# Row maxima of q, k, v and an expert's weights queued one to two ticks later in a fused attention, MoE and GLU kernel

## Chip, cores and metric

The kernel runs on one core of one Trainium2 chip. Its time is the device time in microseconds (us), as the median of several runs. A trace of one profiled execution shows the engines: PE (TensorE matmuls; PEld its weight loads), DVE (VectorE), ACT (ScalarE), POOL (GpSimd) and SP (SyncE, which issues most DMAs here).

## What is computed

The reference is block-causal attention (4 batches, 8 heads, 576 positions, head size 64, blocks of 64), then a mixture of 8 experts whose gate matrix is balanced by 8 row and column normalisations, then a gated unit with silu:

```python
scores = scale * np.matmul(q, k.transpose(0, 1, 3, 2))      # masked by blocks of 64
attn = np.exp(scores - max); attn /= attn.sum(-1)
x = (attn @ v) as (2304, 512)
P = exp(x @ w_gate - max), normalised 8 times over rows and columns
out = sum over e of P[:, e:e+1] * (np.maximum(x @ w1[e], 0) @ w2[e])
g = out @ w_gate2
return (silu(g) * (out @ w_val)) @ w_out
```

## The kernel before

The whole computation is one program. float32 operands of the big products are split into a high and a low float16 part, after a scaling by a power of two that comes from the operand's largest magnitude. The attention phase fills about the first 375 us; the experts' first products (L537) and their weights are already worked on in its gaps. The rest of the program is MoE and GLU.

**Ticks.** A batch has four pairs of heads, so there are 16 pairs p, and each pair has eight ticks u (`NTK = 8`). The generator `attention()` walks over `tk = 8 p + u` and yields three times in a tick; between yields the caller puts in steps of the MoE. In a tick PE makes the scores `s_p_u` (L931 for the first four pairs in float32, L942 from pair 4 on in float16), DVE takes their maxima and makes the bias (L954, L963), ACT one tick later takes the exponentials (L971), DVE two ticks later the reciprocal of the sums (L986 to L991) and POOL scales (L996), PE four ticks later transposes (L1028, copied by ACT at L1029) and then multiplies by v (L1046).

**What is listed at a tick.** A dictionary `events` lists other work by tick, and `at(tick, f, ...)` appends to it. What is listed at a tick is written into the program at the tick's start, ahead of its scores. Every engine runs its instructions in the order in which they are written. For a pair p from 4 on, with r = 8 p, these are listed:

- `load_qk` (L867): SP issues the loads of q (at r-14) and of k (r-13) into `qk0` and `qk1`; each has one buffer, so a load waits until the pair before has done its `lo_qk`.
- `max_qk` (L880): DVE reduces each to a column of magnitudes (r-11 and r-9), and L103 spreads the columns on a diagonal, `qk_d`.
- `across_mid` (L110): PE multiplies the diagonal by ones, which lays the column out as a row in a PSUM bank, `qk_a`. This is the row of maxima.
- `scale_qk` (L116 and behind): DVE reduces the row, gives the bank back, and works out the powers of two.
- `hi_qk` (ACT, L895) and `lo_qk` (DVE, L899): the high and the low part, into `hl0` (q) and `hl1` (k), one buffer each. Behind each `lo_qk` SP issues four DMAs that lay both parts out for the scores: `st0` for q (L910), `st1` for k (L912). The scores of tick r read both.

The scores of u = 0 to 6 and the rows take their PSUM banks in turn from one pool of three, so each takes the bank that was used three takings earlier and waits until that one has been read; u = 7 and the products with v have another bank.

v of the batches after the first is loaded once ahead of its use to find its maximum (`vs`, L831, reduced at L843). The rows of the experts' weights (`w_a`) are written by `across_made` when a caller asks for them and `calm` allows. In the main loop a background generator `w0` works on the first expert's weights and spends a credit of 129 a step.

```python
at(r - 6 + 2 * i, hi_qk, p, i)
at(r - 5 + 1 * i, lo_qk, p, i)
at(r - 8, lambda p: across_mid(st[p]["m"]), p)
at(r - 7, scale_qk, p)
```

Of the kernel before, what the change touches and what calls it, by code (L numbers as in the profile page):

```python
# [30 lines left out]
def attention_moe_glu_kernel(  # L31
# [66 lines left out]
    def across_begin(mx, n, name):  # L98
        pool = pairs[0] if name[0] in "qv" else small
        tag = "dgw" if name[0] == "w" else f"dg{n}"  # L100
        d = pool.tile([P, n, P], F32, tag=tag, name=f"{name}_d", bufs=1)
        for i in range(n):
            nc.vector.tensor_scalar_mul(d[:, i], ident, mx[:, i : i + 1])  # L103
        return {"d": d, "n": n, "name": name}

    def across_mid(g):
        bank, g["free"] = spread[0](g["name"])
        n = g["n"]
        g["row"] = bank[:, : n * P].rearrange("p (n q) -> p n q", n=n)
        nc.tensor.matmul(  # L110
            bank[:, : n * P], ones, g["d"].rearrange("p n q -> p (n q)"), start=True, stop=True
        )
# [8 lines left out]


    soon, row_out, calm, WAIT = [False], [False], [True], 4

    def across_soon(g):
        def mid():
            if "row" not in g and row_out[0]:
                later(1, mid)
            elif "row" not in g:
                across_mid(g)  # L130
                row_out[0] = True

        if soon[0]:
            later(WAIT, mid)

    def across_made(g):
        def made(force):
            if "row" not in g and (force and not row_out[0] or not soon[0] and calm[0]):
                across_mid(g)
                row_out[0] = True  # L140
            return "row" in g

        return made
# [22 lines left out]
    def pow2_scale(mx, n, top, name, root=False):  # L166


        g = across_begin(mx, n, name)
        across_mid(g)  # L170
        return pow2_end(g, n, top, name, root)
# [627 lines left out]
    NTK = len(TICKS)  # L799
# [5 lines left out]
    def attention(actx):  # L805
# [6 lines left out]
        vs, vmx, vt, qk, st, et, xf = {}, {}, {}, {}, {}, {}, {}  # L812
# [7 lines left out]
        def where(p):  # L820
            return p // NPAIR, ORDER[p % NPAIR]
# [3 lines left out]
        def load_v(b, hp, tag, bufs=1):  # L825
            t = tag
            if isinstance(tag, str):
                t = ap.tile([P, NJ, P], F32, tag=tag, name=f"{tag}_{b}_{hp}", bufs=bufs)
            cols = slice(hp * P, (hp + 1) * P)
            nc.gpsimd.memset(t[S - nf * P :, nf], 0.0)  # L830
            nc.sync.dma_start(t[:, :nf], v[b, : nf * P, cols].rearrange("(j p) d -> p j d", p=P))  # L831
            nc.sync.dma_start(t[: S - nf * P, nf], v[b, nf * P :, cols])
            return t
# [80 lines left out]
        def scores(p, u):  # L914
            g = st[p]
            if u == 0:
                for x in ("negm", "bias", "sum", "r"):
                    g[x] = small.tile([P, NC + 1], F32, tag=x, name=f"{x}_{p}")
            if u == NTK - 1:
                sp = ps_x.tile([P, 512], F32, tag="x", name=f"s_{p}_{u}")  # L920
            else:
                sp = ps_s.tile([P, 512], F32, tag="s", name=f"s_{p}_{u}")
            col, places = 0, []
            for c, k0, k1 in TICKS[u]:
                ps = sp[:, col : col + k1 - k0]
                col += k1 - k0
                places.append((c, k0, k1, ps, c if k0 == 0 else NC))
                if p < DIRECT:
                    for h in range(2):
                        a = slice(h * D, (h + 1) * D)  # L930
                        nc.tensor.matmul(  # L931
                            ps[h * CB : (h + 1) * CB],
                            g["q"][a, c * CB : (c + 1) * CB],
                            g["k"][a, k0:k1],
                            start=True,
                            stop=True,
                        )
                    continue
                qs, ks = g["qs"], g["ks"]
                for i in range(2):  # L940
                    for h in range(2):
                        nc.tensor.matmul(  # L942
                            ps[h * CB : (h + 1) * CB],
                            qs[:, h, c * CB : (c + 1) * CB],
                            ks[:, h, i, k0:k1],
                            start=i == 0,
                            stop=i == 1,
                        )
            g["places", u] = places
# [81 lines left out]
        def rest(p):  # L1031

            t = ps_x.tile([P, 512], F32, tag="x", name=f"t_{p}_r").rearrange("p (j q) -> p j q", q=P)
            return self_transpose(p, NC - 1, 4, t)
# [78 lines left out]
        def work(n):  # L1113
            for _ in range(min(n, len(pend))):
                pend.popleft()()

        events = {}

        def at(tick, f, *a):
            events.setdefault(tick, []).append(lambda: f(*a))  # L1120

        for p in range(1, npairs):
            r = p * NTK
            if p < DIRECT:
                if p > 1:
                    at(r - NTK, load_direct, p)
                    at(r - 2, lambda p: vt.update({p: load_v(*where(p), "v", 2)}), p)
                continue
            for i in range(2):
                if p > 1:  # L1130
                    at(r - 14 + 1 * i, load_qk, p, i)
                at(r - 11 + 2 * i, max_qk, p, i)
                at(r - 6 + 2 * i, hi_qk, p, i)
                at(r - 5 + 1 * i, lo_qk, p, i)
            at(r - 8, lambda p: across_mid(st[p]["m"]), p)
            at(r - 7, scale_qk, p)
            at(r - 2, lambda p: vt.update({p: load_v(*where(p), "v", 2)}), p)
        for b in range(B):
            r = (b - 1) * NPAIR * NTK
            for i in range(NPAIR):  # L1140
                if b:
                    at(r + i * NTK + 3, scan_load, b, i)
                at(r + i * NTK + 6 if b else 1 + i, scan_max, b, i if b else ORDER[i])
            r = r + NPAIR * NTK - 2 if b else NPAIR
            at(r, scale_v_begin, b)
            at(r + 1, lambda b: across_mid(vmx[b]), b)
            at(r + 2, scale_v_end, b)

        load_direct(0)
        for p in range(2):  # L1150
# [7 lines left out]
        def on(k):  # L1158
            return 0 <= k < tot

        for tk in range(tot + NTK):
            p, u = divmod(tk, NTK)
            calm[0] = 0 < u < 5
            for f in events.pop(tk, ()):
                f()
            if on(tk):
                scores(p, u)
            if u == 6 and p < npairs:
                take(p, 0, values(p, 0))
            yield  # L1170
            out1 = None
            if on(tk - 4):
                out1 = transposes(*divmod(tk - 4, NTK))
            work(2 if len(pend) > 6 else 1)
            if on(tk - 2):
                normalise(*divmod(tk - 2, NTK))
            if out1:
                out1()
            if on(tk):
                maxima(p, u)  # L1180
            yield

            if p and u == 4:
                work(len(pend))
                take(p - 1, 1, values(p - 1, 1))
                st.pop(p - 1)
                vt.pop(p - 1)
                if p % NPAIR == 0:
                    work(len(pend))
                    ready[0] = p // NPAIR * S // 2  # L1190
            if p and u == 3:
                rest(p - 1)()
            if on(tk - 1):
                exps(*divmod(tk - 1, NTK))
            yield
# [66 lines left out]
    with tc.manual_schedule():  # L1262
# [29 lines left out]
        w0 = Background(0)  # L1292
# [36 lines left out]
        rate, owed, wowed = 47, 0, -9 * 68  # L1329
        with ExitStack() as actx:  # L1330
            yp = actx.enter_context(tc.tile_pool(name="yp", bufs=1))
            for _ in attention(actx):
                wowed += 68
                while wowed >= 3 * 43:
                    w0.step()
                    wowed -= 3 * 43
                if ready[0]:
                    owed += rate
                    while owed >= 3 * NTK * NPAIR:
                        next(fill, None)  # L1340
                        owed -= 3 * NTK * NPAIR
            for _ in fill:
                pass
# [411 lines left out]
```

## Time and profile before

| | |
|---|---|
| median of 3 runs | 2083.08 us (2082.96 to 2089.5) |
| the profiled execution | 2082.69 us, of which the span from its first to its last instruction is 2080.9 us |
| PE busy, over the span | 1954.3 us (94%) |
| DVE busy, over the span | 1618.8 us (78%) |
| ACT busy, over the span | 1379.1 us (66%) |
| mean granted TensorE clock | 0.984 of full speed |

Positions in the rows are microseconds from the span's start. Busy shares over the span are means over very different stretches: in the attention phase neither PE nor DVE is at 94%, as the rows of its stretches below show.

### The profile page before, as it was taken

To read this page: it belongs to the slowest core of one execution; us is meant where nothing else is said; L and a number is where in the kernel's file an instruction comes from. 1 tells how busy PE (TensorE), PEld (TensorE's weight loads), DVE (VectorE), ACT (ScalarE), POOL (GpSimd) and SP (SyncE) were. 2 spreads that over 40 slices of the span, in tenths; PEclk is the share of its full clock that TensorE was granted. 3 is DMA by queue.
4 is the path that set the end of the run, shared out by engine and by line. 5 is a ranking of instruction groups with operands and counts; after the bars stand their busy time and mean duration, and the time that the engine had idled before them with its cause. 6 is when DMAs were issued, how large, how long until landed. Compare 5 with 4: busy or idle time off the path is not lost.

```text
span 2080.9 us, 47230 instructions
## 1 busy us (share of the span) xinstructions
PE 1954.3 (94%) x18378; PEld 1675.8 (81%) x18378; DVE 1618.8 (78%) x3455; ACT 1379.1 (66%) x2940; POOL 611.4 (29%) x871
## 2 busy tenths in 40 slices
PE   7779899799999999999999999999999988999998
PEld 3456666698888888888888888888888877988887
DVE  8886765668887887878878888888887877666666
ACT  6665666348777877777777777777776565544442
POOL 4534444002333333333333333333332223000000
PEclk9799999899999999999999999999999999999999
DMA  4333341306677867878678787777877100301112
GB/s 149 101 101 101 93 116 36 122 22 123 128 173 155 174 127 133 179 150 176 126 134 178 148 173 138 157 152 148 174 149 164 37 11 1 87 22 37 47 42 52
DMA packets 167505, 235.82 MB, mean 113 GB/s; under 512 B 16368, under 2 KB 84464, under 8 KB 167280
## 3 DMA queue, kind: packets, MB, share of 16 engines
q0 software_dynamic: 66560, 107.37, 30.9%
q1 hardware_dynamic: 100720, 125.42, 19.8%
q8 instruction: 144, 2.36, 0.5%
q14 instruction: 81, 0.66, 0.1%
HBM read 90.39 MB, written 24.38 MB: 55 GB/s over the span
## 4 chain that ended last, share of the span: by engine, by line
PE 56%; DVE 15%; ACT 4%; DMA 3%; issue 3%; SPq 0%; POOL 0%; DVEq 0%; ACTq 0%
PE abc_m_b L537 11%; PE m_o_b L645 11%; PE m_o_ac L645 8%; PE abc_m_c L537 5%; PE abc_m_a L537 3%; PE m_go_b L645 3%; PE abc_g_b L537 3%; PE abc_v_b L537 3%; PE m_go_ac L645 2%; DVE m_t L704 2%; DMA wr<-in_w_dram 2%; DVE m_h L193 2%; PE abc_v_c L537 1%; PE abc_g_c L537 1%; DVE w L182 1%
## 5 line engine op out<-in xcount | busy, mean ns | idle before, releaser
L537 PEld LDWEIGHTS <-w 128*128 128x128 f16 x6720 | 610.7, 99 | 111.5 <-issue 46.4
L645 PEld LDWEIGHTS <-m_h 128*128 128x128 f16 x5292 | 514.0, 98 | 68.0 <-issue 9.5
L537 PE MATMUL abc_m_b<-xs,w 128*128 128x256 f16 (+1 forms) x3840 | 478.2, 264 | 31.9 <-DVE m_t L559 29.0
L1444 POOL DMA_DIRECT2D acc<-ev x351 | 305.5, 899 | 584.2 <-ACT ev L1448 365.5
L645 PE MATMUL m_o_b<-w,m_h 128*128 128x256 f16 x3024 | 403.4, 273 | 7.7 <-ACT ev L1448 7.5
L645 PE MATMUL m_o_ac<-w,m_h 128*128 128x256 f16 x2268 | 309.4, 273 | 0.0
L537 PE MATMUL abc_m_c<-xs,w 128*128 128x256 f16 (+1 forms) x1920 | 229.9, 262 | 2.5 <-DVE m_h L758 1.4
L1448 ACT ACTIVATE ev<-m_o_b,pe 128x256 f32<-128x256 f32 x351 | 161.7, 476 | 64.2 <-PE m_o_b L645 52.9
L1448 ACT ACTIVATE ev<-m_o_ac,pe 128x256 f32<-128x256 f32 (+1 forms) x234 | 135.6, 580 | 47.8 <-PE m_o_ac L645 46.4
L178 ACT ACTIVATE w<-wr,ws 128x512 f16<-128x512 f32 x210 | 150.5, 723 | 14.5 <-DVE ws L163 10.7
L182 DVE SCALAR_TENSOR_TENSOR w<-wr,ws,w 128x512 f16<-128x512 f32 x210 | 156.0, 750 | 1.4 <-ACT w L178 1.4
L683 ACT CAST m_h<-m_t 128x512 f16<-128x512 f32 (+1 forms) x210 | 121.8, 580 | 41.6 <-DVE m_t L704 40.7
L1432 POOL DMA_DIRECT2D acc<-ev_s x65 | 73.6, 1132 | 257.0 <-ACT ev_s L1428 257.0
L676 ACT ACTIVATE m_h<-m_t 128x512 f16<-128x512 f32 (+1 forms) x210 | 121.9, 582 | 36.3 <-DVE m_t L574 25.4
L193 DVE TENSOR_TENSOR m_h<-m_t,m_h 128x512 f16<-128x512 f32 (+1 forms) x210 | 133.0, 634 | 8.7 <-ACT m_h L683 8.3
L680 DVE SCALAR_TENSOR_TENSOR m_h<-m_t,m_h 128x512 f16<-128x512 f32 (+1 forms) x210 | 132.1, 634 | 5.8 <-ACT m_h L676 5.6
L537 PEld LDWEIGHTS <-gg_w 128*128 128x128 f16 x1260 | 114.0, 98 | 21.3 <-issue 9.4
L645 PEld LDWEIGHTS <-g_h 128*128 128x128 f16 x1134 | 111.8, 99 | 20.0 <-issue 5.7
L996 POOL TENSOR_SCALAR e<-e,r 128x64 f32<-128x64 f32 (+2 forms) x144 | 77.6, 545 | 159.7 <-DVE r L991 92.7
L537 PEld LDWEIGHTS <-gv_w 128*128 128x128 f16 x1260 | 113.6, 98 | 12.7 <-issue 1.2
L537 PE MATMUL abc_m_a<-xs,w 128*128 128x256 f16 (+1 forms) x960 | 117.5, 262 | 0.0
L600 PEld LDWEIGHTS <-m_h 128*128 128x128 f16 x864 | 83.2, 99 | 16.1 <-issue 6.8
(299 smaller groups left out, 3369.1 us busy)
## 6 DMA issues: line engine op xcount, KB each, us to landing
acc<-ev POOLq DMA_DIRECT2D x351, 256.0 KB, 4.3
wr<-in_w_dram SPq DMA_DIRECT2D x128, 256.0 KB, 4.4
acc<-ev_s POOLq DMA_DIRECT2D x52, 256.0 KB, 4.2
st<-hl SPq DMA_DIRECT2D x48, 144.0 KB, 3.4
raw_g<-in_w_gate_dram SPq DMA_DIRECT2D x12, 512.0 KB, 4.9
raw_v<-in_w_val_dram SPq DMA_DIRECT2D x12, 512.0 KB, 4.6
raw_o<-in_w_out_dram SPq DMA_DIRECT2D x12, 512.0 KB, 4.7
scr_g<-gg SPq DMA_DIRECT2D x21, 256.0 KB, 3.1
```

The costliest lines, as they stand in the source:

```text
L178: nc.scalar.activation(hi, src, AF.Copy, scale=s)
L182: nc.vector.scalar_tensor_tensor(lo, src, s, hi, op0=ALU.mult, op1=ALU.subtract)
L193: nc.vector.tensor_sub(lo, src, hi)
L537: nc.tensor.matmul(ps[:, f], W[o][:, sh, k, f * P : (f + 1) * P], xs[:, o, mh, k, c0 : c0 + n], start=x not in begun, stop=True, skip_grou ...
L600: nc.tensor.matmul(p[:, c * TB : (c + 1) * TB], h[t, r][:, sh, k, ii * P : (ii + 1) * P], W[r, c][:, mh, k], start=c == 0 and j == 0, stop ...
L645: nc.tensor.matmul(ps, h[o][:, sh, k, ii * P : (ii + 1) * P], W[o][:, mh, k], start=o in (X11, X12) and k == 0 and j == 0, stop=True, skip ...
L676: nc.scalar.activation(hi, src, AF.Relu)
L680: nc.vector.scalar_tensor_tensor(lo, src, 0.0, hi, op0=ALU.max, op1=ALU.subtract)
L683: nc.scalar.copy(hi, src)
L996: nc.gpsimd.tensor_scalar(et[c][:, :n], et[c][:, :n], g["r"][:, c : c + 1], 1.0, op0=ALU.mult, op1=ALU.mult)
L1444: nc.gpsimd.dma_start(acc[:, x], e, accum_op=ALU.add)
L1448: nc.scalar.activation(e[:, cols], ps, AF.Copy, scale=p)
```

## The change

Everything that is listed for a pair from the row of maxima on goes one tick later: the row from r-8 to r-7, `scale_qk` from r-7 to r-6, `hi_qk` from r-6 and r-4 to r-5 and r-4, `lo_qk` from r-5 and r-4 to r-4 and r-3. The loads of q and k and their maxima stay where they were. For v of the later batches the row and what is behind it also go one tick later, and the load of `vs` is listed four ticks sooner (except the very first). A row of an expert's weights is now written no earlier than six yields (two ticks) after its diagonal, and no longer in tick 1 of a pair. The credit of `w0` is capped, and a step that can do nothing no longer spends any.

```diff
--- before.py
+++ after.py
@@ -101,7 +101,7 @@
         d = pool.tile([P, n, P], F32, tag=tag, name=f"{name}_d", bufs=1)
         for i in range(n):
             nc.vector.tensor_scalar_mul(d[:, i], ident, mx[:, i : i + 1])
-        return {"d": d, "n": n, "name": name}
+        return {"d": d, "n": n, "name": name, "born": yields[0]}
 
     def across_mid(g):
         bank, g["free"] = spread[0](g["name"])
@@ -121,6 +121,7 @@
 
 
     soon, row_out, calm, WAIT = [False], [False], [True], 4
+    yields = [0]
 
     def across_soon(g):
         def mid():
@@ -135,7 +136,9 @@
 
     def across_made(g):
         def made(force):
-            if "row" not in g and (force and not row_out[0] or not soon[0] and calm[0]):
+            if "row" not in g and (
+                force and not row_out[0] or not soon[0] and calm[0] and yields[0] >= g["born"] + 6
+            ):
                 across_mid(g)
                 row_out[0] = True
             return "row" in g
@@ -1130,21 +1133,21 @@
                 if p > 1:
                     at(r - 14 + 1 * i, load_qk, p, i)
                 at(r - 11 + 2 * i, max_qk, p, i)
-                at(r - 6 + 2 * i, hi_qk, p, i)
-                at(r - 5 + 1 * i, lo_qk, p, i)
-            at(r - 8, lambda p: across_mid(st[p]["m"]), p)
-            at(r - 7, scale_qk, p)
+                at(r - 5 + i, hi_qk, p, i)
+                at(r - 4 + i, lo_qk, p, i)
+            at(r - 7, lambda p: across_mid(st[p]["m"]), p)
+            at(r - 6, scale_qk, p)
             at(r - 2, lambda p: vt.update({p: load_v(*where(p), "v", 2)}), p)
         for b in range(B):
             r = (b - 1) * NPAIR * NTK
             for i in range(NPAIR):
                 if b:
-                    at(r + i * NTK + 3, scan_load, b, i)
+                    at(r + i * NTK + (3 if b == 1 and i == 0 else -1), scan_load, b, i)
                 at(r + i * NTK + 6 if b else 1 + i, scan_max, b, i if b else ORDER[i])
             r = r + NPAIR * NTK - 2 if b else NPAIR
             at(r, scale_v_begin, b)
-            at(r + 1, lambda b: across_mid(vmx[b]), b)
-            at(r + 2, scale_v_end, b)
+            at(r + (2 if b else 1), lambda b: across_mid(vmx[b]), b)
+            events.setdefault(r + (3 if b else 2), []).insert(0, lambda b=b: scale_v_end(b))
 
         load_direct(0)
         for p in range(2):
@@ -1160,7 +1163,7 @@
 
         for tk in range(tot + NTK):
             p, u = divmod(tk, NTK)
-            calm[0] = 0 < u < 5
+            calm[0] = 1 < u < 5
             for f in events.pop(tk, ()):
                 f()
             if on(tk):
@@ -1330,9 +1333,9 @@
         with ExitStack() as actx:
             yp = actx.enter_context(tc.tile_pool(name="yp", bufs=1))
             for _ in attention(actx):
-                wowed += 68
-                while wowed >= 3 * 43:
-                    w0.step()
+                yields[0] += 1
+                wowed = min(wowed + 68, 6 * 43)
+                while wowed >= 3 * 43 and w0.step():
                     wowed -= 3 * 43
                 if ready[0]:
                     owed += rate
```

Line numbers of the changed kernel are 1 higher behind the first edit and 3 higher behind the third: L899 becomes L902, L910 becomes L913, L942 becomes L945. All engines keep the order of their instructions behind the attention phase.

**The queue of SP, ahead of the scores of pair 9.** The names carry the pair: `st0_9` is q of pair 9 for the scores, `st1_9` its k, `qk0_10` and `qk1_10` are the loads of q and k of pair 10, `y0` goes with the gate's work, and `vs_3_0` is later v. Before:

```order
L867 DMA qk0_10_2531<-in_qT_dram 128x576 [waits DMAHW6_49,DVE_49]
L910 DMA st0_9_2562<-hl0_9_2529 64x576 [waits DMAHW7_49,PE_49]
L910 DMA st0_9_2562<-hl0_9_2529 64x576 [waits DMAHW0_49]
L910 DMA st0_9_2562<-hl0_9_2529 64x576 [waits DMAHW1_49]
L910 DMA st0_9_2562<-hl0_9_2529 64x576 [waits DMAHW2_49]
L867 DMA qk1_10_2567<-in_kT_dram 128x576 [waits DMAHW3_49,DVE_49]
L831 DMA vs_3_0_2569<-in_v_dram 128x4x128 [waits DMAHW4_49,Pool_49]
L832 DMA vs_3_0_2569<-in_v_dram 64x128 [waits DMAHW5_49]
L1317 DMA y0_86<-y_10_2527 128x512 [waits DMAHW6_49]
L912 DMA st1_9_2613<-hl1_9_2610 64x1152 [waits DMAHW7_49]
```

Now:

```order
L834 DMA vs_3_0_2361<-in_v_dram 128x4x128 [waits DMAHW5_49,DVE_49]
L835 DMA vs_3_0_2361<-in_v_dram 64x128 [waits DMAHW6_49]
L1320 DMA y0_86<-y_9_2382 128x512 [waits DMAHW7_49,DVE_49]
L870 DMA qk0_10_2533<-in_qT_dram 128x576 [waits DMAHW0_49,DVE_49]
L870 DMA qk1_10_2565<-in_kT_dram 128x576 [waits DMAHW1_49,DVE_49,Activation_49]
L1320 DMA y0_86<-y_10_2521 128x512 [waits DMAHW2_49]
L913 DMA st0_9_2605<-hl0_9_2563 64x576 [waits DMAHW3_49,PE_49]
L913 DMA st0_9_2605<-hl0_9_2563 64x576 [waits DMAHW4_49]
L913 DMA st0_9_2605<-hl0_9_2563 64x576 [waits DMAHW5_49]
L913 DMA st0_9_2605<-hl0_9_2563 64x576 [waits DMAHW6_49]
L915 DMA st1_9_2656<-hl1_9_2610 64x1152 [waits DMAHW7_49]
```

Both loads of pair 10 now stand ahead of the four DMAs of `st0_9`; the load of k stood between the DMAs of `st0_9` and those of `st1_9`. `vs_3_0` stands ahead of all of them. The load `qk1_10` waits in both for DVE's `hl1_9`, which reads the buffer that it fills.

**DVE at the low part of k of pair 9.** `hl1_9` is that low part, `qm_10` the maximum of q of pair 10, which was and is listed three ticks ahead of pair 9. Before:

```order
L899 SCALAR_TENSOR_TENSOR hl1_9_2610<-qk1_9_2152,qk9_s_2471,hl1_9_2610 128x576 [waits DMAHW6_49,DMAHW1_49,DMAHW7_49,DMAHW0_49,Activation_49]
L990 TENSOR_SCALAR r_8_2428<-sum_8_2427 128x1
L991 RECIPROCAL r_8_2428<-r_8_2428 128x1 [waits DVE_49]
L954 TENSOR_REDUCE negm_8_2425<-s_8_4_2618 128x1 [waits PE_49]
L963 TENSOR_SCALAR bias_8_2426<-negm_8_2425,sc_8_2061 128x1 [waits DVE_49]
L1088 TENSOR_TENSOR xf0_6_1_2257<-xf0_6_1_2257 128x5x32 [waits Pool_49]
L193 TENSOR_TENSOR xs_79<-xf1_7_1_2645,xs_79 128x160 [waits Activation_49] x2
L193 TENSOR_TENSOR xs_79<-xf0_6_1_2257,xs_79 128x160 [waits Activation_49]
L880 TENSOR_REDUCE qm_10_2661<-qk0_10_2531 128x1 [waits DMAHW6_49]
```

Now:

```order
L902 SCALAR_TENSOR_TENSOR hl0_9_2563<-qk0_9_2118,qk9_s_2528,hl0_9_2563 128x576 [waits DMAHW4_49,DMAHW5_49,DMAHW3_49,Activation_49]
L993 TENSOR_SCALAR r_8_2414<-sum_8_2413 128x1 [waits Activation_49]
L994 RECIPROCAL r_8_2414<-r_8_2414 128x1 [waits DVE_49]
L957 TENSOR_REDUCE negm_8_2411<-s_8_4_2612 128x1 [waits PE_49]
L966 TENSOR_SCALAR bias_8_2412<-negm_8_2411,sc_8_2116 128x1 [waits DVE_49]
L1091 TENSOR_TENSOR xf0_6_1_2251<-xf0_6_1_2251 128x5x32 [waits Pool_49]
L196 TENSOR_TENSOR xs_79<-xf1_7_1_2639,xs_79 128x160 [waits Activation_49] x2
L196 TENSOR_TENSOR xs_79<-xf0_6_1_2251,xs_79 128x160 [waits Activation_49]
L902 SCALAR_TENSOR_TENSOR hl1_9_2610<-qk1_9_2150,qk9_s_2528,hl1_9_2610 128x576 [waits DMAHW6_49,DMAHW1_49,DMAHW0_49]
L883 TENSOR_REDUCE qm_10_2661<-qk0_10_2533 128x1 [waits DMAHW0_49]
```

The low part of q (`hl0_9`) has taken the place of the low part of k, and `hl1_9` stands one tick further down, directly ahead of the maximum of `qm_10`.

**DVE at the first ticks of pair 9.** `s_9_0` and `s_9_1` are its scores of u = 0 and 1, `qk10_a` the row of maxima of pair 10. Before:

```order
L954 TENSOR_REDUCE negm_9_2794<-s_9_0_2798 128x1
L963 TENSOR_SCALAR bias_9_2795<-negm_9_2794,sc_9_2474 128x2 [waits DVE_49]
L116 TENSOR_REDUCE qk10_r_2833<-qk10_a_2792 128x2
L155 TENSOR_SCALAR qk10_e_2835<-qk10_r_2833 128x2 [waits DVE_49]
L162 TENSOR_SCALAR qk10_i_2837<-qk10_e_2835 128x2 [waits DVE_49]
L163 RECIPROCAL qk10_s_2838<-qk10_i_2837 128x2 [waits DVE_49]
L889 TENSOR_SCALAR sc_10_2841<-qk10_i_2837 128x1
L986 TENSOR_SCALAR r_8_2428<-sum_8_2427 128x1 [waits Activation_49]
L991 RECIPROCAL r_8_2428<-r_8_2428 128x1 [waits DVE_49]
L954 TENSOR_REDUCE negm_9_2794<-s_9_1_2843 128x1 [waits PE_49]
L954 TENSOR_REDUCE negm_9_2794<-s_9_1_2843 128x1
L963 TENSOR_SCALAR bias_9_2795<-negm_9_2794,sc_9_2474 128x2 [waits DVE_49]
```

Now:

```order
L957 TENSOR_REDUCE negm_9_2796<-s_9_0_2800 128x1
L966 TENSOR_SCALAR bias_9_2797<-negm_9_2796,sc_9_2531 128x2 [waits DVE_49]
L989 TENSOR_SCALAR r_8_2414<-sum_8_2413 128x1 [waits Activation_49]
L994 RECIPROCAL r_8_2414<-r_8_2414 128x1 [waits DVE_49]
L957 TENSOR_REDUCE negm_9_2796<-s_9_1_2837 128x1 [waits PE_49]
L957 TENSOR_REDUCE negm_9_2796<-s_9_1_2837 128x1
L966 TENSOR_SCALAR bias_9_2797<-negm_9_2796,sc_9_2531 128x2 [waits DVE_49]
L116 TENSOR_REDUCE qk10_r_2868<-qk10_a_2835 128x2
```

The reduction of the row (L116), which gives its bank back, stood ahead of the reciprocal at L986 and of the maxima of `s_9_1`, and now stands behind them. On PE the row itself has gone from directly ahead of `s_9_0` to directly ahead of `s_9_1`, and `s_9_2` now takes its bank.

## Rows read from the trace of the kernel before

**Rows 1.** Windows of the attention phase: us, then busy us (instructions) by engine, clock.

```profile
52.00:104.00 52.00, 38.57 (x251) 21.31 (x251) 43.32 (x140) 31.59 (x85) 27.51 (x60) 0.77 0.36 101
...
156.00:208.00 52.00, 49.36 (x470) 36.17 (x470) 34.72 (x122) 31.17 (x85) 24.47 (x59) 1.00 0.35 101
```

**Rows 2.** Waits of PE, 15 to 364 us: total us, times, longest.

```profile
PE w_a L110 <- DVE r L990: 5.9, 1, 5.9
...
PE qk_a L110 <- DVE qk_d L103: 4.1, 4, 1.9
PE qk_a L110 <- DVE r L990: 4.0, 3, 2.1
...
PE v_a L110 <- DVE r L990: 2.8, 1, 2.8
PE w_a L110 <- DVE w_d L103: 1.6, 2, 1.0
```

**Rows 3.** Waits of DVE, the same stretch.

```profile
DVE hl L899 <- ACT hl L895: 8.5, 10, 2.4
...
DVE vmx L843 <- DMA vs<-in_v_dram: 4.5, 3, 2.0
```

**Rows 4.** Windows across the longest wait of PE, columns as in the first group.

```profile
124.00:127.00 3.00, 0.08 (x1) 0.00 (x0) 2.46 (x6) 1.24 (x5) 0.65 (x2) 1.00 0.84 214
127.50:134.00 6.50, 4.07 (x22) 2.68 (x23) 5.69 (x20) 2.33 (x4) 0.69 (x1) 0.50 0.00 0
```

**Rows 5.** Timeline of SP ahead of pair 9: start, us, line, operation, tiles, count.

```profile
195.09 0.34 SPq L867 DMA_DIRECT2D qk<-in_kT_dram  x1
...
197.31 0.58 SPq L1317 DMA_DIRECT2D y<-y  x1
197.93 2.39 SPq L912 DMA_DIRECT2D st<-hl  x4
```

**Rows 6.** Issue to landing of the DMAs of L912, 190 to 205 us.

```profile
DMA to landing us min/median/max: 2.8/2.8/2.9
```

**Rows 7.** Timeline of DVE around the same place; in brackets idle before and its releaser.

```profile
194.25 0.82 DVE L899 SCALAR_TENSOR_TENSOR hl<-qk,qk_s,hl 128x576 f16<-128x576 f32 x1 [0.77 <-ACT hl L895]
...
198.03 0.74 DVE L880 TENSOR_REDUCE qm<-qk 128x1 f32<-128x576 f32 x1
...
204.51 0.42 DVE L116 TENSOR_REDUCE qk_r<-qk_a 128x2 f32<-128x256 f32 x1
...
207.97 0.33 DVE L963 TENSOR_SCALAR bias<-negm,sc 128x2 f32<-128x2 f32 x1
```

**Rows 8.** Timeline of PE at the first ticks of pair 9.

```profile
203.50 0.37 PE L942 MATMUL s<-st,st 128*64 128x64 f16 x8
...
207.40 0.46 PE L942 MATMUL s<-st,st 128*64 128x320 f16 x4
```

**Rows 9.** Timeline of DVE, where the low part of k of pairs 7, 10, 11, 13 will stand.

```profile
146.68 0.74 DVE L880 TENSOR_REDUCE qm<-qk 128x1 f32<-128x576 f32 x1
...
216.18 0.74 DVE L880 TENSOR_REDUCE qm<-qk 128x1 f32<-128x576 f32 x1
...
237.76 0.74 DVE L880 TENSOR_REDUCE qm<-qk 128x1 f32<-128x576 f32 x1
...
289.17 0.74 DVE L880 TENSOR_REDUCE qm<-qk 128x1 f32<-128x576 f32 x1
```

**Rows 10.** Timeline of PE, first scores of these pairs (of 10 the row ahead).

```profile
153.01 0.36 PE L942 MATMUL s<-st,st 128*64 128x64 f16 x8
...
224.62 0.70 PE L110 MATMUL qk_a<-qk_d,ones 128*128 128x256 f32 x2 [2.06 <-DVE r L990]
...
244.07 0.37 PE L942 MATMUL s<-st,st 128*64 128x64 f16 x8
...
294.20 0.37 PE L942 MATMUL s<-st,st 128*64 128x64 f16 x8
```

**Rows 11.** Waits of SP, 15 to 364 us.

```profile
SPq L867 <- DVE hl L899: 91.7, 10, 17.2
```

## Prediction

> **What bounds the kernel now.** The edits reach only the attention phase: all engines keep the order of their instructions behind it. So I read that phase alone, and what its end moves by is what the kernel moves by. I began with windows along it. In 52 to 104 us DVE is busy for 43.32 of 52 us (83%), PE for 38.57 us, and at a granted clock of 0.77; in 156 to 208 us PE is busy for 49.36 us (95%) at full clock and DVE for 34.72 us (67%) [rows 1]. So the early stretch follows DVE, and from about pair 7 on PE sets the pace: there a microsecond that PE waits is a microsecond of the kernel, and a microsecond that DVE saves is none.
>
> Next I read what PE waits for. The row matmuls of L110 wait in all for 5.9 + 4.1 + 4.0 + 2.8 + 1.6 = 18.4 us [rows 2], nearly a third of it in one place, the row of an expert's weights that ends at 129.9 us. PE waits there because the row is written directly behind the DVE instructions that make its diagonal. DVE waits too: 8.5 us for the high part that ACT writes in the same tick, and 4.5 us for `vs` to land [rows 3]. Then I read the queue of SP, since `lo_qk` feeds the scores through eight DMAs, and there lies what I think decides. SP stands for 91.7 us in ten waits at a load of L867 until DVE has done a low part [rows 11]; nothing behind it is issued in that time.
>
> **The change part by part.** Durations are from the profiled execution (2082.69 us, 0.4 us below the median of 2083.08), and the sum is made against its time.
>
> *Rows later: a gain.* The diagonal is done a tick before its row is wanted, so I take the waits of L110 for gone. What they are worth depends on the stretch. Of the 18.4 us, 5.9 lie at the weights' row. In 124 to 127 us, while PE stands, DVE is busy for 2.46 of 3.0 us [rows 4]: the wait is DVE's work and much of it comes back elsewhere. Its bounds are 0 and 5.9; I take 3.2, a little over half. Of the other 12.5 us, some 7 lie ahead of 104 us, in the stretch in which DVE is at 83%. Bounds 0 and 7; I take 1.5, about the part of DVE's own 13.0 us of waits (8.5 + 4.5) that can fall on four of twelve pairs and isn't filled with other work. The rest lies directly ahead of first scores from pair 7 on, and is settled below, with what takes its place. Gain: 4.7 us.
>
> *Low parts later: the load of k in front of the scores' DMAs.* This is the rule of the queue that I weigh most. Before, SP issued the four DMAs of `st0`, then the load of the next pair's k, then those of `st1`. Now the load of k stands ahead of all eight, and it still waits for DVE's low part of k, one tick later than before. So no DMA of q either leaves until the low part of k is done, though q's was ready a tick earlier. From the start of `hl1_9`, the last DMA lands after: the low part 0.82 us [rows 7], the load of k 0.34 and some 0.1 to the next [rows 5], four of `st0` at the length that the four of `st1` show, 2.39, three more of `st1` 1.8 [rows 5], and 2.8 to landing [rows 6]. That is 8.25 us; where a `y` of 0.58 us [rows 5] stands among them (pairs 9 and 13), 8.85.
>
> Its start is about that of the L880 beside it, which had that place before. Against the first scores of the pair:
>
> - pair 9: 198.03 [rows 7] + 8.85 = 206.9; PE wanted it at 203.50 [rows 8]: 3.4 us late
> - pair 13: 289.17 [rows 9] + 8.85 = 298.0; wanted at 294.20 [rows 10]: 3.8 late
> - pair 11: 237.76 [rows 9] + 8.25 = 246.0; wanted at 244.07 [rows 10]: 1.9 late
> - pair 7: 146.68 [rows 9] + 8.25 = 154.9; wanted at 153.01 [rows 10]: 1.9 late
> - pair 10: 216.18 [rows 9] + 8.25 = 224.4. PE stood ready 2.06 us ahead of 224.62, waiting for the row [rows 10], so at 222.6: 1.9 late, in place of the 2.06 that goes. Net nothing. I take pair 14 for the same, by its like place in a batch.
>
> At the other pairs I find the DMAs in time, or late by less than the row's wait that goes. The sum is 3.4 + 3.8 + 1.9 + 1.9 = 11.0 us. DVE no longer waits for ACT ahead of the low part (0.77 us at pair 9 [rows 7]), so it may begin up to 0.8 sooner at each of the four, which leaves 7.8. I take the middle, 9.4 us. The same DMAs were in time before because half of them had left a tick earlier.
>
> The Trainium skill speaks against this change here: its page DMA: Bandwidth & Descriptors (Anatomy of one DMA) says that DMA engines don't wait on semaphores, and that every such wait stands on the issuing sequencer, ahead of the dispatch. The 91.7 us of SP at L867 agree with it [rows 11]. If a waiting load let those behind it pass, this term would be near nothing, and the sum about 2083.
>
> *The row's bank.* `s_9_2` now takes the bank of the row, and L116, which gives it back, stands behind the bias of u = 1. That bias ended at 207.97 + 0.33 = 208.30, and with L116's 0.42 the bank is back at 208.72 [rows 7], while PE took up `s_9_2` at 207.40 [rows 8]: 1.3 us late. Where the first scores already waited for DMAs (pairs 7, 9, 11, 13), the exponentials that DVE waits for in front of that bias are done meanwhile, and little is left. At pairs 10 and 14 I take the whole, at the other eight 0.3 each, for this is worth nothing where DVE is ahead or the pace is its own: 2 × 1.3 + 8 × 0.3 = 5.0. Bounds are 0 and 12 × 1.3 = 15.6; the one row that I have belongs to a pair where it is mostly hidden, so I stay nearer the low one.
>
> *The rest.* `vs` is issued four ticks sooner, and DVE's 4.5 us go; they are among the 13.0 above. Its two DMAs take room on SP's queue ahead of the loads, where SP only waits (the 91.7 us cover them; without that cover the two would cost about 1 us a pair). The maxima of q may wait for a load that now leaves only a tick sooner; PE has work in that time. The credit and the rule on `calm` move steps of the first expert's weights inside the phase: the same instructions, so 0, with 2 us either way.
>
> Sum: 2082.7 − 4.7 + 9.4 + 5.0 = 2092.4, and with the 0.4 to the median 2092.8.
>
> **The rivals.**
>
> *The waits go and nothing takes their place: faster.* DVE loses 13.0 us of waits, so it may come to the listed tick earlier against PE than the rows say; it decides from the point at which its lead at pairs 9 and 13 has grown by 3.4 to 3.8 us. Then the DMAs are in time, and L110's waits are gain. In full that is 2083.1 − 18.4 = 2064.7; as part of them lies in DVE's stretch, half of it, 2083.1 − 9.2 = 2074, is what I would expect. For it: DVE waits for much beside PE. Against it: from pair 7 on DVE's position follows PE's scores, whose maxima it takes, so both shift together and the distance stays.
>
> *Gain and loss cancel: no change.* With the bank at nothing and the DMAs at the low end: 2083.1 − 4.7 + 7.8 − (up to 4 from waits of PE for ACT that a stall makes shorter) = 2082 to 2086. For it: a stall of PE lets ACT and DVE catch up.
>
> *The clock follows the stalls: much slower.* After the wait of 5.9 us the granted clock was 0.50 for 6.5 us, that is 1.2 in place of 2.4 GHz, and PE was busy for 4.07 us of them [rows 4]: about 2.0 us of work lost. Should each of the four stalls bring such a stretch, 4 × 2.0 = 8 come on top: 2101; with every term at its upper bound about 2110. The Trainium skill (TensorE: Matmul & The Clock Gate, What's actually happening) has activity alone release the clock, and idle time bring it back to 1.2 GHz, which the fall after 124 us bears out; whether a stall of 3.4 us is enough no row here settles.
>
> **How the numbers follow.** A measurement of this kernel can tell 0.3%, 6.2 us, from no change. I give the forecast (2088 to 2098) 0.42, the clock 0.13, cancelling 0.22 and faster 0.23. The likeliest gives 2092.8. The range reaches from 2072, which leaves out some 0.1 at the fast end, to 2104, which leaves out less than 0.1. Slower by over 0.3% (beyond 2089.3) holds most of the forecast and the clock: 0.51. Within 0.3%: the cancelling case and the edges of its neighbours, 0.28. Faster: 0.21.
>
> **What would show it.** Right: L110 hardly waits; PE's first scores of pairs 7, 9, 11 and 13 wait for `st` DMAs, by 1.9 to 3.8 us; on SP the DMAs of `st0` and `st1` leave in one run behind the load of k; `s_10_2` waits for L116. Wrong in the gain: PE still stands at L110, or DVE's busy share in 52 to 104 us does not rise. Wrong in the loss: the last `st` lands ahead of the first scores' place, or PE's stalls are made good by shorter waits for ACT behind them. The end of the attention phase against 375 us tells the sum, for nothing behind it has moved.

## The result, and the profile after

The changed kernel takes 2104.16 us (median; 2103.55 to 2108.48) against 2083.08 us of before (2082.93 to 2091.99): slower by 21 us, a ratio of 1.0106 with a 95% interval from 1.0087 to 1.0125. The forecast was 2092.8 us, in 2072 to 2104. The direction was right and the size about half. The profiled execution of the changed kernel took 2108.48 us, with a span of 2106.7 us; that of before took 2082.69 us, so the two traces lie 25.8 us apart, some 5 us more than the medians.

All of it comes out of the attention phase. The first store of the experts' output is a mark behind that phase; this is its row before and after (line, count, duration, and the first and the last start):

```profile
L1444 POOL DMA_DIRECT2D acc<-ev x351: 847/856/1549, 475.5 to 1596.3; - x176
```

```profile
L1447 POOL DMA_DIRECT2D acc<-ev x351: 847/856/1549, 503.1 to 1621.7; - x176
```

The first store starts 27.6 us later and the last 25.4 us later: what is lost is there at 503 us, and the rest of the program gives back only 2. The windows of the changed kernel:

```profile
52.00:104.00 52.00, 34.19 (x232) 17.65 (x230) 38.59 (x129) 29.54 (x82) 24.68 (x53) 0.77 0.28 77
156.00:208.00 52.00, 45.97 (x395) 33.81 (x394) 33.49 (x106) 26.89 (x75) 19.83 (x49) 0.93 0.34 90
```

In 52 to 104 us DVE, which set the pace there, fell from 43.32 to 38.59 us of work; in 156 to 208 us PE did 45.97 in place of 49.36 us, at a granted clock of 0.93 where it had been 1.00 [rows 1]. The waits of PE in the attention phase (total us, times, longest):

```profile
PE s L945 <- DMA st<-hl: 24.5, 14, 3.1
...
PE qk_a L110 <- ACT e L974: 5.3, 1, 5.3
...
PE s L945 <- DVE qk_r L116: 2.1, 4, 0.7
...
PE w_a L110 <- ACT e L974: 0.6, 1, 0.6
PE v_a L110 <- DVE r L993: 0.5, 1, 0.5
```

The row matmuls wait for 6.4 us where they waited for 18.4 [rows 2]; in their place the scores wait for 24.5 us for the DMAs of `st`, of which the kernel before has none among its waits. They lie at the first scores of eight pairs, in two pieces each at six of them (start, duration; in brackets idle before, and its releaser):

```profile
77.32 0.23 PE L945 MATMUL s<-st,st 128*64 128x64 f16 x1 [2.29 <-DMA st<-hl]
78.52 0.48 PE L945 MATMUL s<-st,st 128*64 128x64 f16 x7 [0.96 <-DMA st<-hl]
...
110.95 0.21 PE L945 MATMUL s<-st,st 128*64 128x64 f16 x1 [2.73 <-DMA st<-hl]
112.29 0.50 PE L945 MATMUL s<-st,st 128*64 128x64 f16 x7 [1.13 <-DMA st<-hl]
...
164.71 0.19 PE L945 MATMUL s<-st,st 128*64 128x64 f16 x1 [3.09 <-DMA st<-hl]
166.19 0.50 PE L945 MATMUL s<-st,st 128*64 128x64 f16 x7 [1.28 <-DMA st<-hl]
...
220.12 0.21 PE L945 MATMUL s<-st,st 128*64 128x64 f16 x1 [2.92 <-DMA st<-hl]
221.41 0.50 PE L945 MATMUL s<-st,st 128*64 128x64 f16 x7 [1.08 <-DMA st<-hl]
221.84 1.46 PE L540 MATMUL abc_m_c<-xs,w 128*128 128x256 f16 x6
...
266.37 0.19 PE L945 MATMUL s<-st,st 128*64 128x64 f16 x1 [2.49 <-DMA st<-hl]
267.68 0.50 PE L945 MATMUL s<-st,st 128*64 128x64 f16 x7 [1.12 <-DMA st<-hl]
...
320.87 0.19 PE L945 MATMUL s<-st,st 128*64 128x64 f16 x1 [2.94 <-DMA st<-hl]
322.14 0.50 PE L945 MATMUL s<-st,st 128*64 128x64 f16 x7 [1.08 <-DMA st<-hl]
```

These are pairs 4, 5, 7, 9, 11 and 13; pairs 10 and 14 waited once each, for 0.45 and 0.98 us. Early in the phase DVE has a new wait as well, for the weights' loads, which stand behind the run of eight DMAs on SP:

```profile
DVE wmx L378 <- DMA wr<-in_w_dram: 6.2, 2, 4.8
```

On DVE and SP the chain of pair 9 reads as it was forecast. DVE first, then SP:

```profile
212.53 0.86 DVE L902 SCALAR_TENSOR_TENSOR hl<-qk,qk_s,hl 128x576 f16<-128x576 f32 x1
```

```profile
213.46 0.33 SPq L870 DMA_DIRECT2D qk<-in_kT_dram  x1
213.84 0.42 SPq L1320 DMA_DIRECT2D y<-y  x1
214.35 2.43 SPq L913 DMA_DIRECT2D st<-hl  x4
216.83 2.52 SPq L915 DMA_DIRECT2D st<-hl  x4
```

The load of k leaves when the low part of k is done, and then all eight DMAs of `st` in one run; the second piece of PE's wait ends at 221.41, 8.9 us after the low part began (8.85 in the forecast). Behind the stall the clock falls:

```profile
219.00:225.60 6.60, 4.40 (x25) 3.44 (x26) 0.65 (x3) 1.99 (x5) 0.28 (x1) 0.54 0.57 150
```

That is 1.2 GHz for nearly all of 6.6 us, and six matmuls like those that took 0.82 us at 216.39 take 1.46 at 221.84.

### The profile page after: what moved, and what is told of

It is laid out like the page before. It is cut to its first block, busy times and chain, and to the rows that moved or that the text cites. A ratio compares the mean times of both kernels' runs of the same rounds, so it can differ in the third digit from the quotient of the medians.

```text
span 2106.7 us, 47220 instructions
## 1 busy us (share of the span) xinstructions
PE 1960.0 (93%) x18378; PEld 1679.4 (80%) x18378; DVE 1621.2 (77%) x3455; ACT 1379.0 (65%) x2940; POOL 613.5 (29%) x871
## 4 chain that ended last, share of the span: by engine, by line
PE 54%; DVE 16%; ACT 4%; issue 3%; DMA 3%; SPq 0%; POOL 0%; DVEq 0%; ACTq 0%
PE abc_m_b L540 11%; PE m_o_b L648 11%; PE m_o_ac L648 8%; PE abc_m_c L540 5%; PE abc_m_a L540 3%; PE abc_g_b L540 3%; PE abc_v_b L540 3%; PE m_go_b L648 3%; PE m_go_ac L648 2%; DVE m_t L707 2%; DVE m_h L196 2%; DMA wr<-in_w_dram 2%; PE abc_v_c L540 1%; DVE w L185 1%; PE abc_g_c L540 1%
## 5 line engine op out<-in xcount | busy, mean ns | idle before, releaser
L648 PEld LDWEIGHTS <-m_h 128*128 128x128 f16 x5292 | 514.0, 98 | 68.3 <-issue 9.8
L185 DVE SCALAR_TENSOR_TENSOR w<-wr,ws,w 128x512 f16<-128x512 f32 x210 | 156.1, 752 | 1.5 <-ACT w L181 1.5
L648 PEld LDWEIGHTS <-g_h 128*128 128x128 f16 x1134 | 110.4, 98 | 18.4 <-issue 5.4
L378 DVE TENSOR_REDUCE wmx<-wr 128x1 f32<-128x512 f32 x128 | 85.7, 680 | 19.1 <-DMA wr<-in_w_dram 19.0
```

Of the source, the lines that this page charges most:

```text
L185: nc.vector.scalar_tensor_tensor(lo, src, s, hi, op0=ALU.mult, op1=ALU.subtract)
L378: nc.vector.tensor_reduce(g["mx"][:, k : k + 1], g["b"][k // 2][k % 2], axis=AX.XY, op=ALU.max, apply_absolute_value=True)
L648: nc.tensor.matmul(ps, h[o][:, sh, k, ii * P : (ii + 1) * P], W[o][:, mh, k], start=o in (X11, X12) and k == 0 and j == 0, stop=True, skip ...
```

## The experiments

Each edit is against the changed kernel where nothing else is said; ratios are to the kernel before on the same chip (0.001 is 2.1 us).

**The load of k behind q's DMAs again (e1_k_load_later).**

```diff
-                    at(r - 14 + 1 * i, load_qk, p, i)
+                    at(r - 14 + 2 * i, load_qk, p, i)
```

> The changed kernel, with the load of the next pair's k listed one tick later, so that on SP it again stands behind the four DMAs of st0 and not ahead of all eight. Theory (queue): the time was lost because q's four DMAs stand behind a load that waits for the low part of k. The last DMA then lands some 2.4 us sooner, the waits of PE's first scores for st fall from 24.5 us to under 10, the stretches at half clock behind them go in part, and the time falls from 2104 to 2086 to 2093. Rival (lateness): the low part of k itself comes too late, whatever stands ahead; the waits stay above 18 us and the time above 2099. Rival (bank): the scores of u = 2 that wait for L116 carry the loss; time unchanged within 3 us.

Measured: 2090.17 us, 1.0043 (1.0030 to 1.0057), some 13 us of the 21. The wait for `st`, and SP around pair 9:

```profile
PE s L945 <- DMA st<-hl: 9.4, 11, 1.2
```

```profile
198.83 3.15 SPq L913 DMA_DIRECT2D st<-hl  x4
202.33 0.33 SPq L870 DMA_DIRECT2D qk<-in_kT_dram  x1
202.71 2.38 SPq L915 DMA_DIRECT2D st<-hl  x4
```

Four of the eight DMAs leave ahead of the load again, the waits fall by 15.1 us and the time by 13 to 14, as the theory of the queue had it. Lateness is not nothing: e2_low_parts_early, the next run, has the same order on SP with the low parts a tick sooner, and is another 12 us faster. So the order on the queue carries about half of what the late low parts cost. The Trainium skill's rule (DMA: Bandwidth & Descriptors, Anatomy of one DMA) that a wait stands on the issuing sequencer, which the page gives under the path of GpSimd, is what this edit tries on SP. The trace agrees: the four DMAs of L913 left 0.9 us behind the load (213.46 and 214.35) and now leave 3.5 us ahead of it (198.83 and 202.33).

**The low parts at their old ticks (e2_low_parts_early).**

```diff
-                at(r - 4 + i, lo_qk, p, i)
+                at(r - 5 + i, lo_qk, p, i)
```

> The changed kernel, with the low parts (and so their DMAs) back at the ticks at which they stood before, r-5 and r-4; the row of maxima and the reduction behind it stay one tick later. Theory (queue): no wait of the first scores for st is left (under 3 us of 24.5), the row's waits stay gone, and the time comes to 2075 to 2084, by whether the bank's late return costs the 5 us that were forecast. Rival (bank): the time stays above 2090, with waits of scores for L116. Rival (DVE): DVE waits 8 us and more for the high parts again and the time lies at 2083 to 2090.

Measured: 2078.18 us, 0.9984 (0.9971 to 0.9997). This one line is worth 25 us, and what is left of the change (the later rows, the sooner `vs`, the weights' rows and the credit) makes the kernel slightly faster than before.

```profile
PE s L945 <- DVE qk_r L116: 2.6, 5, 0.7
...
PE s L945 <- DMA st<-hl: 1.0, 2, 0.7
```

```profile
DVE hl L902 <- ACT hl L898: 11.2, 10, 2.0
```

The wait for `st` is all but gone, the row's waits stay gone, and DVE waits for ACT's high parts again, for 11.2 us in place of 8.5 [rows 3]. The time lies below the 2083 to 2090 us that the rival gave for these waits, so that rival falls; what they cost by themselves no run here shows.

**The loads of later v at their old ticks (f1_vs_old_place).**

```diff
-                    at(r + i * NTK + (3 if b == 1 and i == 0 else -1), scan_load, b, i)
+                    at(r + i * NTK + 3, scan_load, b, i)
```

> The changed kernel, with the loads of later v back at their old ticks, behind the loads of q and k. Theory (queue): what blocks SP is the load of k, vs only stands ahead of it while SP waits anyway; time 2101 to 2107. Rival (vs): the early loads of vs hold SP or the buffer and delay all behind them; time under 2097.

Measured: 2117.59 us, 1.0168 (1.0141 to 1.0195), 13 us slower than the changed kernel. Both theories missed.

```profile
215.34 0.33 SPq L870 DMA_DIRECT2D qk<-in_kT_dram  x1
215.76 0.39 SPq L834 DMA_DIRECT2D vs<-in_v_dram  x1
216.21 0.51 SPq L835 DMA_DIRECT2D vs<-in_v_dram  x1
216.77 0.58 SPq L1320 DMA_DIRECT2D y<-y  x1
217.44 2.60 SPq L913 DMA_DIRECT2D st<-hl  x4
```

```profile
PE s L945 <- DMA st<-hl: 27.0, 17, 4.3
```

```profile
DVE vmx L846 <- DMA vs<-in_v_dram: 11.0, 6, 3.1
```

At the old tick the loads of `vs` come behind the waiting load of k and ahead of the eight DMAs: at pair 9 they hold these back by 1.0 us. PE's waits for `st` grow by 2.5 us, and DVE waits for `vs` for 11.0 us. The sooner load of `vs` is what kept the changed kernel from being worse.

**Only the rule on the weights' rows and the credit (f3_weight_rows_only)**, on the kernel before; with the sooner `vs` as well (**f5_weight_rows_and_vs**).

> The kernel before, with only the rule on the rows of the experts' weights (six yields after the diagonal, not in tick 1) and the credit changed; q, k and v stay at their old ticks. Theory: the wait of 5.9 us at the weights' row goes, worth 0 to 5.9; time 2077 to 2084. Rival: the edits on the weights carry a part of the loss (DVE's waits for the weights' loads, 6.2 us in the changed kernel); time above 2087.

> The kernel of f3_weight_rows_only, with the loads of later v four ticks sooner as well; rows of q, k and v stay at their old ticks. Theory (queue): DVE's 4.5 us of waits for vs go and are worth at most that, 2083 to 2087. Rival (vs): sooner v is worth more than DVE's waits, under 2080.

Measured: 2086.94 us, 1.0022 (1.0006 to 1.0039), and 2085.19 us, 1.0006 (0.9995 to 1.0017). The wait of 5.9 us at the weights' row is gone in both and gives nothing back; f3_weight_rows_only loses 0.0022 against its theory, at the edge of what its rival had. The sooner `vs` is worth 3 us, no more than DVE's waits, by intervals that overlap.

**The reduction in the row's own tick (g1_reduce_same_tick)**, on e2_low_parts_early, and on the changed kernel (**i1_late_same_tick**).

```diff
-            at(r - 6, scale_qk, p)
+            at(r - 7, scale_qk, p)
```

> The kernel of e2_low_parts_early, with the reduction of the row (L116) listed in the row's own tick, r-7, so that it again stands ahead of the reciprocal and of the maxima of u = 1, and the bank is back before the scores of u = 2 want it. Theory (bank): the scores' waits for L116 (2.6 us for q and k) go, and with them up to 5 us, the term of the forecast: 2073 to 2077 beside 2078.2. Rival (pace elsewhere): those waits lie beside DVE's own and nothing is gained, within 1.5 us of 2078. Rival (DVE): DVE now waits for the row at L116, a row matmul of some 0.7 us for each pair, and the time rises by 3 to 8 us.

> The changed kernel, with the reduction of the row in the row's own tick, so that the bank of u = 2 comes back early; low parts stay late. Theory (bank): the waits of scores for L116 go and with them the 2 to 4 us that the same edit gave with early low parts: 2100 to 2102. Rival (the forecast's term): 5 us, 2099. Rival (hidden): in the changed kernel those scores come behind a stall, and nothing is gained, 2103 to 2106.

Measured: 2077.19 us, 0.9971 (0.9953 to 0.9988), 3 us less than e2_low_parts_early, within the two intervals, so that neither the gain nor the rival of no gain is shown; and 2104.45 us, 1.0097 (1.0070 to 1.0123), the changed kernel's own within them. In the changed kernel the bank cost nothing that can be measured: PE still waited 25.2 us for `st`, and DVE now waited for the row:

```profile
PE s L945 <- DMA st<-hl: 25.2, 15, 3.2
```

```profile
DVE qk_r L116 <- PE qk_a L110: 8.8, 3, 3.7
```

**The old credit (g2_credit_old)**, on e2_low_parts_early, and on the changed kernel (**f2_credit_old**).

```diff
-                wowed = min(wowed + 68, 6 * 43)
-                while wowed >= 3 * 43 and w0.step():
+                wowed += 68
+                while wowed >= 3 * 43:
+                    w0.step()
```

> The kernel of e2_low_parts_early, with the credit of the background steps as it was before (a step that can do nothing spends it, and it isn't capped). Theory: the credit only places the steps of the first expert's weights and costs nothing: within 2 us of 2078.2. Rival: the new credit makes the steps come in a bunch and holds DVE in 52 to 104 us, which is what the weights' edits alone lost (0.22%): time 2073 to 2076.

> The changed kernel, with the credit of the background steps as before. On the kernel with early low parts the old credit gave 0.3%. Theory: the new credit alone costs 4 to 7 us in every kernel, by where it puts steps in 52 to 104 us; here too, 2097 to 2100 beside 2104. Rival (hidden): PE and DVE wait for the low parts' DMAs anyway and the credit is worth nothing, 2102 to 2106.

Measured: 2074.20 us, 0.9954 (0.9935 to 0.9973), 6 us less than e2_low_parts_early by intervals that just touch, as the rival had it; and 2103.43 us, 1.0093 (1.0058 to 1.0128), no difference that can be told from the changed kernel, so that the theory of 4 to 7 us in every kernel missed. DVE in 52 to 104 us, with the new credit and with the old:

```profile
52.00:104.00 52.00, 36.95 (x261) 19.62 (x262) 42.86 (x139) 32.70 (x90) 27.02 (x59) 0.84 0.37 105
```

```profile
52.00:104.00 52.00, 40.95 (x297) 22.99 (x296) 45.76 (x152) 34.84 (x95) 27.65 (x63) 0.84 0.38 106
```

With the old credit DVE is busy for 45.76 in place of 42.86 us in the stretch that it paces, most of the difference with the weights (L378 4.0 in place of 2.6 us, L185 3.1 in place of 2.3). That this is what the 6 us come from is argued and not shown; in the changed kernel, where the scores wait for their DMAs, none of it shows in the time. The wait of PE at the weights' row is back in all three kernels with the old credit, in g2_credit_old so:

```profile
PE w_a L110 <- DVE w_d L103: 6.2, 1, 6.2
```

**v at its old ticks with early low parts (g5_vs_old_place), and no age rule (g3_no_age_rule)**, both on e2_low_parts_early.

> The kernel of e2_low_parts_early, with the loads of later v back at their old ticks. In the changed kernel that cost 13 us, as the loads then stood behind the eight late DMAs and DVE waited 11.0 us for them. Theory (queue): here SP is not held up, DVE's wait is the old 4.5 us, and the time rises by 1 to 4 us. Rival (vs): sooner v is worth the 13 us by itself, whatever stands ahead; 2088 and more.

> The kernel of e2_low_parts_early, without the rule that a row of an expert's weights is written six yields after its diagonal (tick 1 of a pair stays barred). Theory: that rule takes a wait of PE for DVE's diagonal away that lies in DVE's own stretch, so its worth is 0 to 3 us; without it 2078 to 2082. Rival: the whole 5.9 us of that wait come back, 2084.

Measured: 2085.74 us, 1.0005 (0.9987 to 1.0022), 4 us slower than e2_low_parts_early, by intervals that overlap; and 2078.58 us, 0.9975 (0.9960 to 0.9990), the same as it. So most of the 13 us of f1_vs_old_place belong to `vs` together with the blocked queue. (The first expectation has those loads behind the eight DMAs; the rows of f1_vs_old_place have them ahead.) The age rule (the six yields behind the diagonal) is worth nothing here, and it is not what took the wait at the weights' row away, for without it that wait stays short:

```profile
PE w_a L110 <- ACT e L972: 0.6, 1, 0.6
```

With the rule and the old credit it is 6.2 us; with the new credit all such waits come to 0.6 us, with the rule (e2_low_parts_early) and without it. So here the credit decides it. That a row is now written six yields behind its diagonal, as the section on the change says, does not keep PE from waiting for that diagonal.

**The gains together (h1_early_same_credit):** early low parts, reduction in the row's tick, old credit.

> Row one tick later and its reduction in the same tick, low parts at their old ticks, credit as before; v and the weights' rows as in the changed kernel. Theory (the gains add): 0.9954 of before from the credit and a further 0.1% from the bank, 0.994, 2071 to 2074. Rival (they overlap, both lie in DVE's stretch): no better than either alone, 2074 to 2077.

Measured: 2073.41 us, 0.9945 (0.9927 to 0.9962), the fastest of all, 11 us under before. It is not told apart from g2_credit_old by the intervals, so that the gains add is not shown.

## Why the prediction was right, and where it was wrong

**The row's waits.** They went, as said (18.4 to 6.4 us; the 5.3 of what is left lies at pair 4, behind a stall that is new). What they are worth where nothing takes their place shows between f5_weight_rows_and_vs and g1_reduce_same_tick, which differ only by the later rows (of q, k and v, with v's reduction) and the later high part of q. PE's waits at L110 fall from 13.3 us (7.7 + 2.2 + 2.1 + 1.3) to 5.4 (3.1 + 2.1 + 0.2), and the time by 7 us (1.0006 to 0.9971, with intervals that lie apart). Their longest lines, first f5_weight_rows_and_vs:

```profile
PE qk_a L110 <- DVE r L993: 7.7, 5, 2.6
```

```profile
PE qk_a L110 <- ACT e L974: 3.1, 1, 3.1
```

That e2_low_parts_early stands 3.3 us under before (0.0016), close to the sum of the terms −4.7 and +5.0, is luck: it also holds the new credit, which costs some 6 us there, the sooner `vs`, and the rows ahead of first scores from pair 7 on, which the 4.7 leaves out. The parts of the 4.7 were wrong as well. The 3.2 us for the weights' row did not come (f3_weight_rows_only), and g2_credit_old and h1_early_same_credit, the two fastest kernels, have that wait, 6.2 us long: it is DVE's work, and the lower bound, 0, was the value to take. One sign named for a wrong gain came too: DVE's busy time in 52 to 104 us did not rise (43.32 us before, 38.59 now, 42.86 in e2_low_parts_early).

**The low parts' DMAs: the step that failed.** The mechanism was right: one run of eight DMAs behind a load that waits for the low part of k. The term was 9.4 us and measured 25 (1.0106 less 0.9984, 0.0122 of 2083 us). Two things in it were too small, and a third, the clock behind the stalls, was left out of it and put down as a rival.

- The pairs. The step counted pairs 7, 9, 11 and 13 and found the DMAs "in time, or late by less than the row's wait that goes" elsewhere. The four waited for 16.0 us, where 11.0 were worked out and 9.4 taken; pairs 4, 5, 10 and 14 waited for 8.5 us more, of which 3.3 at pair 4 and 3.9 at pair 5. I had set the landing against the place where PE stood ready before, and the phase's early part did not keep those places. At pair 4 the low part began at 70.26, near the 69.64 of the L880 whose place it took, but PE stood ready 4.8 us behind that start where it had been 8.2: the row waits ahead of these scores had gone. At pair 5 DVE came late to the low part in turn (103.27; the L880 of before at 95.72), after its new wait of 6.2 us for the weights' loads, which wait on the same queue.
- The size. Pair 7 waited for 4.4 us in place of 1.9. From the start of its low part, 156.17, to PE's second piece, 166.19, it is 10.0 us in place of 8.25: the low part took 1.10 us and the issue of the four DMAs of L915 3.84, where the rows of pair 9 gave 0.82 and 2.39. And PE stood ready 5.5 us behind that start in place of 6.3. A landing from a place on DVE's old timeline holds only if DVE keeps it, and here DVE had waited for 1.93 us for ACT's `m_h` just ahead. At pair 9, where I had the rows, 4.0 stood against 3.4 and the chain's length against its estimate, 8.9 and 8.85. That DVE would begin up to 0.8 us sooner against PE, for which the step took off 1.6 us, came at none of the four pairs.

The start of the low part and PE's first scores at pair 4 (before, then now), and the low part and the DMAs of L915 at pair 7:

```profile
69.64 0.74 DVE L880 TENSOR_REDUCE qm<-qk 128x1 f32<-128x576 f32 x1
...
78.43 0.62 PE L942 MATMUL s<-st,st 128*64 128x64 f16 x8 [0.57 <-DVE v_e L155]
```

```profile
70.26 0.81 DVE L902 SCALAR_TENSOR_TENSOR hl<-qk,qk_s,hl 128x576 f16<-128x576 f32 x1
...
156.17 1.10 DVE L902 SCALAR_TENSOR_TENSOR hl<-qk,qk_s,hl 128x576 f16<-128x576 f32 x1
```

```profile
160.22 3.84 SPq L915 DMA_DIRECT2D st<-hl  x4
```

From the changed kernel to e1_k_load_later the waits for `st` fall by 15.1 us and the time by 13 to 14; from there to e2_low_parts_early by 8.4, and the time by 12. The clock rises along with them, so how much of a stall is made good behind it is not shown.

**The bank.** 5.0 us were forecast. In the changed kernel i1_late_same_tick shows nothing; with early low parts it is about 3, within the intervals. The thought that a stall at the first scores hides it fits this, applied to more pairs; but DVE's new wait of 8.8 us for the row in i1_late_same_tick could hide a gain as well, and no run separates the two.

**The credit** was set at 0 with 2 us either way. It costs about 6 with early low parts, with intervals that just touch, and nothing that shows in the changed kernel.

**The rivals.** The clock did follow the stalls, which I gave 0.13: 0.54 in 219 to 225.6 us, after PE had stood for 2.92 and 1.08 us. The rule of the Trainium skill (TensorE: Matmul & The Clock Gate, What's actually happening) that idle time brings 1.2 GHz back agrees with it. Of the four cases this rival's 2101 us lay nearest to the result. How many of the 25 us are the clock's no run here separates, for no kernel had the stalls without it. An estimate comes from one long stretch of the changed kernel and of e2_low_parts_early:

```profile
104.00:390.00 286.00, 247.12 (x2143) 175.80 (x2142) 192.41 (x604) 171.69 (x453) 115.27 (x253) 0.93 0.33 86
```

```profile
104.00:390.00 286.00, 254.54 (x2343) 185.64 (x2342) 199.70 (x633) 178.78 (x471) 112.98 (x258) 0.98 0.35 101
```

The granted clock is lower by 0.05 over 247 us of PE's work, which is some 12 us, and at most that, as PE doesn't set the pace everywhere. In e1_k_load_later, whose waits are shorter than 1.3 us each, it is 0.97. The figure of about 2110 us for every term at its upper bound doesn't come out of the bounds given: 2082.7 + 11.0 + 15.6 + 8 without a gain is 2117.

The rival "the waits go and nothing takes their place" is e2_low_parts_early, and it gained 3 us, not 9; with the old credit besides (g2_credit_old) it gained about 10.

## What to carry to other kernels

Before an operation is moved a tick later, follow every DMA that it issues through its queue, and look for a waiting transfer that now stands ahead of them: here one load's place was worth 13 us. When a stall is found at one step of a repeated pattern, count it at every repetition until a row excludes it; slack read from the old timeline wasn't kept here. A long wait of an engine that another engine's work fills can be worth nothing: here it stands in the two fastest kernels.

## What I had not expected

Loads of 0.9 us of issue time (`vs`), placed behind a blocked transfer rather than ahead of it, cost 13 us in one kernel and 4 us, within the intervals, in another that differs by the place of the low parts alone. And a background generator's credit, which only places steps, went with about 6 us and with the coming and going of PE's longest row wait.
